# Attention and two gated MLPs on one core: the work list of the first two blocks is written anew

## The chip, the cores and the metric

The kernel runs on one core of a Trainium2 chip. The metric is the time of one execution on the device in microseconds (us). Before the change three runs gave 1640.0, 1640.85 and 1644.39 us, a median of 1640.85 us.

## What is computed

```python
def _attn_ref(q, k, v, g_norm):                    # 8 x 8 heads, 576 positions, 64 wide
    kv = np.einsum('bhsd,bhse->bhde', k, v)        # "k'v": one 64x64 matrix per head
    out = np.einsum('bhsd,bhde->bhse', q, kv)
    rms = np.sqrt(np.mean(out * out, axis=-1, keepdims=True) + 1e-06)
    return out / rms * g_norm
def _moe_ref(x, w_gate, w_val, w_out):             # 4608 tokens, 512 -> 1536 -> 512
    return (1 / (1 + np.exp(-(x @ w_gate))) * (x @ w_val)) @ w_out
def _moe2_ref(x, w_in, w_out):                     # 512 -> 2048 -> 512
    h = x @ w_in
    return np.where(h >= 1, h, np.where(h <= -1, 0, (h + 1) ** 2 / 4)) @ w_out
```

The reference applies the three one after the other. The weights of the two MLPs come as float64.

## The kernel before

The 4608 tokens are worked through in 9 blocks of 512. A block is held with the 512 features on partitions, as four tiles of 128x512, one for each pair of heads. Large products are exact to float32 with a trick: both operands are split into a high and a low half, and three products (high-high, high-low, low-high, `mm3`, lines 92 to 96) are added in PSUM.

For a block the attention goes like this. `kv_heads` multiplies k by v for the pairs (128-position chunks, 64x64 results), the result is copied to SBUF (`kvw`), `attn_two` multiplies it with q to X, two tiles of 128x512 in PSUM. The squares of X are summed over each head, the sums become reciprocal roots (the norm), these are spread again over 64 partitions by a small product (`scale_steps`, result R), and x = X times g_norm times R is split into halves. The first MLP then multiplies x with 12 columns of weights `f`; each column has a gate half and a value half (`gv_chunk`, four chunks of three products each), and the sigmoid of the gate times the value is stored in DRAM.

The first two blocks (0 and 1) are special. Nothing can be hidden behind earlier work there, so the steps of both blocks, the decoding of the first three weight columns from float64 (`dec`, six VectorE steps per tile) and the first products are written out by hand as a list of names, `order` in the text. Each name is a generator, and each time that it stands in the list one step of it is issued. `kv10` is k'v of block 1, pair 0; `X10` is X of block 1, pairs 0 and 1; `sq`, `sum`, `norm`, `turn`, `scale`, `split` are the steps of the norm; `W0110` is weight column 0, block 1, value half (1), chunk 0; `g01` is the sigmoid of column 0, block 1. Every engine runs its own instructions strictly in the order in which they are issued, so the list sets which instruction of an engine stands behind which.

The first block's norm and the second's are made differently before the change. For block 0 the squares are multiplied, as the stationary operand, with a matrix of two columns (`early_sums`, line 285): four products of two columns for each pair, tokens on partitions, so that the six steps of the norm work on 32 columns. `early_turn` (line 308) turns the 8 rows back. For block 1 the squares are split into halves (`half`), multiplied with a 0/1 matrix `gather` (`middle_squares`, line 323, two products of 512 columns per pair), and the norm steps work on 512 columns (`middle_norm`).

The inputs are loaded through one queue, SyncE's (SP), in the order of the text: block 0's k, v, rest, q for each pair, then the weights of column 0, block 1's, then columns 1 and 2. A load waits for the eighth load before it. POOL's queue stores the split weights to DRAM (`store_resident`) for later stages, where they are read back. After the list, a loop over `f` = 1 to 11 runs columns 1 to 11 for block 1 and 2 to 11 for block 0 (`first`), while VectorE decodes column f+2.

Of the kernel before, what the change touches and what calls it, by code (L numbers as in the profile page):

```python
# [15 lines left out]
P = 128  # L16
# [17 lines left out]
def attn_gated_mlp_kernel(ctx: ExitStack, tc: tile.TileContext, a: dict, out: bass.AP):  # L34
# [273 lines left out]
    def early_turn(j):  # L308
        rt = bank("R", 1, "rt", (H, T))
        for c in range(TC):  # L310
            nc.tensor.matmul(rt[:, c * P:(c + 1) * P], state[j][:, c, :], eye, start=True, stop=True)
        yield
        hi, lo = (tp.tile([H, T], F32R, name=f"rt_{n}", tag=n) for n in ("sqh", "sql"))
        yield from split_steps(rt, hi, lo)
        state[j] = hi, lo
# [141 lines left out]
    def store_resident(f):  # L457

        d = w1d[f]
        store_halves(wgv[f, 0], [d[:, 0:2, h] for h in range(2)])  # L460
        store_halves([t[:, 2 * P:] for t in wgv[f, 1]], [d[:, 2, h] for h in range(2)])
# [94 lines left out]
    def store_halves(halves, dst):  # L556
        for t, d in zip(halves, dst):
            t = t.bitcast(F32)
            nc.gpsimd.dma_start(out=d, in_=t if len(d.shape) == 2 else t.rearrange("p (o n) -> p o n", n=2 * P))  # L559
# [495 lines left out]
    with tc.manual_schedule():  # L1055
# [57 lines left out]
        square_tags = (("sq", "sqh", "gf", "sig"), ("gf", "sig", "nm", "nr"))  # L1113
        high_tags, low_tags = ("nt", "woh", "woh", "sq"), ("wol", "wol", "qraw", "qraw")
        two = ("woh", "wol", "qraw")
        gv_banks = {(0, 0): (None, None), (1, 0): (2, 1), (0, 1): (None, None)}

        class Early:

            def kv(b, p):  # L1120
                if p % 2 == 0:
                    kvb[b, p // 2] = at_p.tile([P, 2, D], F32, name="kvps", tag="at")
                kv_heads(kvb[b, p // 2], b, p)
# [10 lines left out]
            def X(b, i):  # L1134
                attn_two(b, i, None if b == i == 1 else [acc_tile(c, "X") for c in ((0, 1) if i else (2, 3))])
# [10 lines left out]
            def half(b, p):  # L1146
                hi, lo = (half_tile(tp, "sqh", t[p], bufs=2 if t[p] in two else 1) for t in (high_tags, low_tags))
                yield from split_steps(state[b, p], hi, lo)
                state[b, p] = hi, lo
# [11 lines left out]
            def scale(b, p):  # L1161
                bank = acc_tile((0, 3)[p] if b else p % 2, "R") if b == 0 or p < 2 else at_tile("R")
                yield from scale_steps(b, p, bank, state["x", b, p])
# [22 lines left out]
            def W(f, b, i, c):  # L1186
                if c == 0:
                    gb[f, b, i] = gv_bank(i, gv_banks[f, b][i])
# [19 lines left out]
        def feed(n):  # L1208
# [6 lines left out]
            kv00 kv01 kvw00 X00 sq00 x00 sq01 x01 kv02 sum00 kv03 kvw01 X01 dec00 cast dec00 dec00 sum01 dec00 sq03 sq02 x02  # L1215
            dec01 dec00 sum02 dec00 dec01 w00 dec01 dec01 sum03 kv10 norm0 norm0 kv11 norm0 dec01 norm0 dec01 norm0 kvw10
            norm0 w01 w00 turn0 x03 w01 X10 turn0 turn0 scale00 sq11 x10 scale01 half11 scale00 kv12 sq10 scale01 scale02
            kv13 split00 half11 kvw11 split00 half10 X11 scale02 split01 dec10 half10 W0010 sq13 split01 sum10 sq12 dec10
            W0000 dec10 half12 sum11 dec10 half13 scale03 half12 split02 half13 dec11 sum12 dec10 sum13 dec11 dec10 W0001
            split02 w10 norm1 W0011 dec11 norm1 w10 W0002 norm1 scale03 W0012 norm1 split03 norm1 W1000 dec11 split03 W1001  # L1220
            norm1 dec11 norm1 dec11 W1002 norm1 W0003 w11 W0013 scale10 w11 W1003 x11 W1010 scale10 scale11 x12 g00 W1011
            scale11 split10 dec20 scale12 split11 W1012 split10 scale12 x13 dec21 scale13 W1013 split12 g00 g10 W0100
            split11 W0110 scale13 W0101 split12 split13 W0111 split13 W0102 g10 W0112 dec20 W0113 dec20 dec21 W0103 dec21
            dec20 g01 dec20 dec20 g01 w20 dec21 dec21 w20 dec21 w21 w21
# [335 lines left out]
```

## Time and profile before

| | |
|---|---|
| median of three runs | 1640.85 us (1640.0 to 1644.39) |
| the profiled execution | 1640.12 us; its span, first to last instruction, 1638.3 us |
| TensorE matmul (PE) busy | 1621.2 us, 99% of the span |
| VectorE (DVE) / ScalarE (ACT) / GpSimd (POOL) busy | 71% / 55% / 11% |
| TensorE clock, mean | 0.996 of full speed |
| last product of weight columns 0 for block 1 ends, and block 2's first k'v starts | 66.93 us from the start |

The span counts from the first instruction to the last one; the execution's own time has 1.8 us more around it. A busy time of PE says only that a product was under way. All of the change lies in the first 70 us.

### The profile page before, as it was taken

Reading aid. Unit: us, or ns where it says so; the run is one execution under the profiler, and the core shown is the slowest. Engines: PE = TensorE matmul, PEld = TensorE weight load, DVE = VectorE, ACT = ScalarE, POOL = GpSimd, SP = SyncE. Lnnn points to the kernel's source line nnn. Section 1 sums busy time; section 2 is a strip of 40 time slices with the busy share of each in tenths; the row PEclk is TensorE's granted clock in tenths of the full one; section 3 lists DMA queues with packets and bytes.
Section 4 is the critical chain, followed back from the end, with each engine's and each line's share of the span. In section 5 each row is a group of like instructions: output and inputs, shape, how many; then the busy total and the mean of one; then the engine's idle time right before and its main releaser. Section 6 shows DMA issues by size and latency. Waiting matters only on the chain.

```text
span 1638.3 us, 22607 instructions
## 1 busy us (share of the span) xinstructions
PE 1621.2 (99%) x8060; PEld 1355.5 (83%) x8060; DVE 1159.8 (71%) x1726; ACT 901.9 (55%) x1384; POOL 186.7 (11%) x292
## 2 busy tenths in 40 slices
PE   8999999999999999999999999999999999999999
PEld 6778878887788777788888788888888888999999
DVE  5987876786786667676666646965795588479476
ACT  3444445765774457744433456646754675575563
POOL 0112042211211111210221100000000000000000
PEclk8999999999999999999999999999999999999999
DMA  9676797678985998859985876558655755777855
GB/s 286 213 262 234 225 317 255 203 270 299 364 320 175 330 330 318 284 195 332 349 307 192 286 272 232 186 190 297 201 199 204 277 186 202 286 274 260 320 179 193
DMA packets 146575, 422.07 MB, mean 258 GB/s; under 512 B 18200, under 2 KB 25496, under 8 KB 132384
## 3 DMA queue, kind: packets, MB, share of 16 engines
q1 hardware_dynamic: 125536, 353.51, 63.9%
q0 software_dynamic: 20928, 67.13, 11.0%
q8 instruction: 64, 1.05, 0.3%
q14 instruction: 47, 0.39, 0.1%
HBM read 337.20 MB, written 83.36 MB: 257 GB/s over the span
## 4 chain that ended last, share of the span: by engine, by line
PE 62%; issue 26%; POOL 6%; DMA 3%; DVE 2%; ACT 1%; SPq 0%; POOLq 0%; DVEq 0%; ACTq 0%
PE bank L836 21%; PE bank L996 21%; PE pA L672 5%; PE acc L96 3%; PE acc L94 3%; PE acc L95 3%; PE pF L672 2%; POOL w1d L559 2%; POOL w2d L559 1%; POOL wo2d L559 1%; PE pD L672 1%; PE h L94 1%; PE h L95 1%; PE h L96 1%; DMA woh<-wo1d 1%
## 5 line engine op out<-in xcount | busy, mean ns | idle before, releaser
L996 PE MATMUL bank<-gh,wo 128*128 128x512 f32 (+1 forms) x1680 | 345.8, 367 | 0.0
L996 PEld LDWEIGHTS bank<-gh,wo 128*128 128x128 f32 x1680 | 305.8, 188 | 39.2
L69 ACT ACTIVATE gh<-g 128x1024 fp32r<-128x1024 f32 (+2 forms) x171 | 155.5, 912 | 135.8 <-PE bank L996 99.2
L672 PE MATMUL pA<-xc,wc 128*128 128x512 f32 x828 | 212.0, 391 | 1.9 <-ACT pD L69 1.3
L836 PE MATMUL bank<-x_t,wst 128*128 128x512 f32 (+1 forms) x960 | 210.0, 367 | 0.0
L836 PEld LDWEIGHTS bank<-x_t,wst 128*128 128x128 f32 x960 | 175.2, 188 | 22.4
L672 PEld LDWEIGHTS pA<-xc,wc 128*128 128x128 f32 x828 | 154.4, 188 | 36.6 <-ACT pD L69 2.6
L771 DVE TENSOR_TENSOR gh<-g,gh 128x1024 fp32r<-128x1024 f32 (+1 forms) x140 | 156.0, 1115 | 29.7 <-ACT gh L69 29.4
L69 ACT ACTIVATE kept<-bank 128x512 f32<-128x512 f32 (+1 forms) x200 | 109.3, 549 | 95.2 <-PE bank L836 82.0
L94 PE MATMUL acc<-gh,woh 128*128 128x512 f32 x404 | 158.2, 392 | 2.9 <-DMA woh<-wo1d 2.3
L836 PE MATMUL bank<-x_b,wst 128*128 128x512 f32 (+1 forms) x720 | 160.8, 367 | 0.0
L771 DVE TENSOR_TENSOR g<-bank,kept 128x512 f32<-128x512 f32 (+1 forms) x160 | 98.1, 634 | 84.4 <-ACT kept L69 45.8
L95 PE MATMUL acc<-gl,woh 128*128 128x512 f32 x404 | 157.5, 390 | 0.1
L836 PEld LDWEIGHTS bank<-x_b,wst 128*128 128x128 f32 x720 | 131.5, 188 | 16.9
L886 DVE SCALAR_TENSOR_TENSOR g<-r,g 128x1024 f32<-128x1024 f32 (+1 forms) x70 | 78.0, 1114 | 73.1 <-ACT r L883 73.1
L96 PE MATMUL acc<-gh,woh 128*128 128x512 f32 x308 | 120.2, 390 | 0.0
L880 ACT ACTIVATE r<-g,half 128x1024 f32<-128x1024 f32 (+1 forms) x70 | 74.4, 1064 | 65.3 <-DVE g L771 65.3
L672 PE MATMUL pF<-xc,wc 128*128 128x512 f32 x432 | 109.7, 389 | 0.0
L672 PEld LDWEIGHTS pF<-xc,wc 128*128 128x128 f32 x432 | 81.0, 188 | 17.2 <-issue 0.4
L94 PEld LDWEIGHTS acc<-gh,woh 128*128 128x128 f32 x404 | 75.8, 188 | 20.7 <-ACT nm L69 1.4
L95 PEld LDWEIGHTS acc<-gl,woh 128*128 128x128 f32 x404 | 75.8, 188 | 16.1 <-DVE gl L77 0.5
L771 DVE TENSOR_TENSOR g<-g 128x1024 f32<-128x1024 f32 (+1 forms) x80 | 88.6, 1113 | 0.5
(221 smaller groups left out, 2559.2 us busy)
## 6 DMA issues: line engine op xcount, KB each, us to landing
wo<-wo2d SPq DMA_DIRECT2D x70, 1024.0 KB, 5.0
wc<-w1d SPq DMA_DIRECT2D x252, 256.0 KB, 5.5
woh<-wo1d SPq DMA_DIRECT2D x162, 256.0 KB, 5.4
wst<-w2d SPq DMA_DIRECT2D x40, 1024.0 KB, 5.5
wst<-w2d SPq DMA_DIRECT2D x40, 768.0 KB, 4.5
raw<-in_w SPq DMA_DIRECT2D x32, 512.0 KB, 6.0
raw<-in_w_gv SPq DMA_DIRECT2D x24, 512.0 KB, 5.4
w1d<-w2half POOLq DMA_DIRECT2D x48, 256.0 KB, 4.4
```

Of the source, the lines that this page charges most:

```text
L69: nc.scalar.activation(out=o, in_=i, func=AF.Copy)
L94: nc.tensor.matmul(ps, w[0][:, wsl], x[0], start=first, stop=False)
L95: nc.tensor.matmul(ps, w[0][:, wsl], x[1], start=False, stop=False)
L96: nc.tensor.matmul(ps, w[1][:, wsl], x[0], start=False, stop=last)
L559: nc.gpsimd.dma_start(out=d, in_=t if len(d.shape) == 2 else t.rearrange("p (o n) -> p o n", n=2 * P))
L672: nc.tensor.matmul(o, w[:, h, sl], x[c][l], start=first and c == n == 0, stop=c == 1 and n == 2, skip_group_check=True)
L771: nc.vector.tensor_tensor(out=o, in0=x, in1=y, op=op)
L836: nc.tensor.matmul(bank, self.ws[w][h][:, sl], self.xo[x][:, l, c], start=first and c == n == 0, stop=c == 1 and n == 2, skip_group_check= ...
L880: nc.scalar.activation(out=r, in_=v, func=AF.Relu, bias=self.half, scale=0.5)
L886: nc.vector.scalar_tensor_tensor(out=v, in0=r, scalar=1.0, in1=v, op0=ALU.min, op1=ALU.max)
L996: nc.tensor.matmul(bank[i][o], self.wo2[2 * i + k // 2][:, k % 2 * 2 + e, h, o * P:(o + 1) * P], ops[m][:, l, e], start=first, stop=k == H ...
```

## The change

Five things change, all at the beginning. (1) The list of names stands in another order. (2) The sums of block 1's squares are made as block 0's are, with `early_sums`, `early_norm` and `early_turn`; `half`, `middle_squares` and `middle_norm` are no longer used for block 1. (3) X is copied out of PSUM, times g_norm, by ScalarE in place of VectorE, for six of the eight pairs. (4) k and v of one pair come in one load into the ring `raw` of six buffers, which the raw weights share. (5) k'v of block 1 is made for two pairs at a time, with the products of the two pairs alternating. Besides, the banks of PSUM are given out differently (column 0 and column 1 of block 0 both use h1 and h0), and the four stores of weight column 0 move from POOL's queue to SP's; there they are issued in the loop after the list, as before in the text.

```diff
     def load_kv_early(b, p):
-        k, v, r = (wp.tile([P, T], F32, name="kv_early", tag="w") for _ in range(3))
-        k, v = (x[0:SC].rearrange("p (c n) -> p c n", c=NSC) for x in (k, v))
-        r = r[0:SR, 0:2 * P].rearrange("p (i n) -> p i n", i=2)
-        nc.sync.dma_start(out=k, in_=a["kv_main"][b, p][:, 0])
-        nc.sync.dma_start(out=v, in_=a["kv_main"][b, p][:, 1])
+        t = tp.tile([SC, 2, NSC, P], F32, name="kvraw", tag="raw", bufs=6)
+        nc.sync.dma_start(out=t, in_=a["kv_main"][b, p])
+        r = wp.tile([P, T], F32, name="kv_early", tag="w")[0:SR, 0:2 * P].rearrange("p (i n) -> p i n", i=2)
         nc.sync.dma_start(out=r, in_=a["kv_rest"][b, p])
-        kvraw[b, p] = k, v, r
+        kvraw[b, p] = t[:, 0], t[:, 1], r
...
-        nc.vector.tensor_scalar(out=x, in0=X, scalar1=gn, scalar2=None, op0=ALU.mult)
+        if j == 0 and p < 2:
+            nc.vector.tensor_scalar(out=x, in0=X, scalar1=gn, scalar2=None, op0=ALU.mult)
+        else:
+            nc.scalar.activation(out=x, in_=X, func=AF.Copy, scale=gn)
...
-            state[j] = bank("R", 0, "SSt", (P, TC, H))
+            state[j] = bank("R", 2 * j, "SSt", (P, TC, H))
...
-        rt = bank("R", 1, "rt", (H, T))
+        rt = bank("R", 1 + j, "rt", (H, T))
...
     def store_resident(f):
         d = w1d[f]
+        queue = nc.gpsimd if f else nc.sync
...
-        gv_banks = {(0, 0): (None, None), (1, 0): (2, 1), (0, 1): (None, None)}
+        scale_banks = (("h0", "at", "at", "h0"), ("at", "at", 0, 1))
+        gv_banks = {(0, 0): ("h1", "h0"), (0, 1): (0, 1), (1, 0): ("h1", "h0")}
...
-                kv_heads(kvb[b, p // 2], b, p)
+                kv_heads(kvb[b, p // 2], b, *((p, p + 1) if b else (p,)))
...
-                (middle_squares if b else early_sums)(b, p)
+                early_sums(b, p)
...
-                yield from (middle_norm if b else early_norm)(b)
+                yield from early_norm(b)
...
-            kv00 kv01 kvw00 X00 sq00 x00 sq01 x01 kv02 sum00 kv03 kvw01 X01 dec00 cast dec00 dec00 sum01 dec00 sq03 sq02 x02
+            kv00 kv01 kvw00 X00 kv02 x01 sq00 sq01 x00 kv03 sum00 kvw01 dec00 X01 dec00 dec00 sum01 sq02 dec00 sq03 sum02
...
```

Three places of the new order matter for what follows. The first is TensorE's queue around the first block's norm: `SSt` are the two-column sums of squares, `rt` is the turn, `R` the spread, `kvps` is k'v, `X` the attention product. Before:

```order
L290 MATMUL SSt<-ones_169,sq 128x2 x12
L159 MATMUL kvps<-kv_early 64x64 x20
L311 MATMUL rt<-eye,early_r 8x128 x4
L186 MATMUL X<-q_early,kvw_174 64x64 x4
L186 MATMUL X<-q_early,kvw_175 64x448 x4
L319 MATMUL R<-rt_sqh,spread 128x512
L319 MATMUL R<-rt_sql,spread 128x512
```

And now:

```order
L291 MATMUL SSt<-ones_169,sq 128x2 x12
L312 MATMUL rt<-eye,early_r 8x128 x4
L157 MATMUL kvps<-kvraw 64x64 x8
L157 MATMUL kvps<-kv_early 64x64 x2
L157 MATMUL kvps<-kvraw 64x64 x8
L157 MATMUL kvps<-kv_early 64x64 x2
L320 MATMUL R<-rt,spread 128x512 x8
L184 MATMUL X<-q_early,kvw_174 64x64 x4
L184 MATMUL X<-q_early,kvw_175 64x448 x4
L94 MATMUL h<-xh_455,w 128x512
```

The turn now stands ahead of block 1's first k'v, all four spreads follow at once, and X of block 1 comes after them; the first weight product is the next thing.

The second place is TensorE's queue where the weight products (`h`) begin. Before, block 1's squares are summed there with `SSh`, of 512 columns:

```order
L94 MATMUL h_538<-xh_511,w 128x512
L95 MATMUL h_538<-xl_512,w 128x512
L96 MATMUL h_538<-xh_511,w 128x512
L328 MATMUL SSh<-sqh,gather 128x512 x2
L94 MATMUL h_551<-xh_511,w 128x512
L95 MATMUL h_551<-xl_512,w 128x512
L96 MATMUL h_551<-xh_511,w 128x512
L328 MATMUL SSh<-sqh,gather 128x512 x2
L319 MATMUL R<-rt_sqh,spread 128x512
L319 MATMUL R<-rt_sql,spread 128x512
L328 MATMUL SSh<-sqh,gather 128x512 x4
```

Now the sums are `SSt`, and the second X of block 1 stands among them:

```order
L291 MATMUL SSt<-ones_169,sq 128x2 x4
L184 MATMUL X<-q_early,kvw_174 64x64 x4
L184 MATMUL X<-q_early,kvw_175 64x448 x4
L291 MATMUL SSt<-ones_169,sq 128x2 x4
L94 MATMUL h<-xh_473,w 128x512
L95 MATMUL h<-xl_474,w 128x512
L96 MATMUL h<-xh_473,w 128x512
L291 MATMUL SSt<-ones_169,sq 128x2 x8
```

The work of block 1 up to its sums has moved behind the first weight products.

The third place is TensorE's queue at the first product of weight column 1 (the rows show the numbers of the tiles and what an instruction waits for). Before, it writes `h0_613`, a bank of its own, while columns 0 are in `h0_551` and `h1_538`:

```order
L94 MATMUL h1_538<-xh2_569,w_445 128x512
L95 MATMUL h1_538<-xl2_570,w_445 128x512
L96 MATMUL h1_538<-xh2_569,w_446 128x512
L94 MATMUL h0_613<-xh0_511,w_587 128x512 [waits Activation_49]
L95 MATMUL h0_613<-xl0_512,w_587 128x512
L96 MATMUL h0_613<-xh0_511,w_588 128x512 [waits DVE_49]
```

And now (`h_625` is the gate of column 1; it takes the bank of `h_480`, the gate of column 0):

```order
L312 MATMUL rt_597<-eye_172,early_r_576 8x128 [waits DVE_49,PE_49]
L312 MATMUL rt_597<-eye_172,early_r_576 8x128 x3
L94 MATMUL h_480<-xh3_541,w_391 128x512
L95 MATMUL h_480<-xl3_542,w_391 128x512
L96 MATMUL h_480<-xh3_541,w_392 128x512
L94 MATMUL h_515<-xh3_541,w_448 128x512
L95 MATMUL h_515<-xl3_542,w_448 128x512
L96 MATMUL h_515<-xh3_541,w_449 128x512
L94 MATMUL h_625<-xh0_455,w_565 128x512 [waits Activation_49]
```

The first product of column 1 now stands two chunks behind the second turn and waits for ScalarE. On ScalarE the copy of the turn, a table load and the sigmoid that reads `h_480` follow each other:

```order
L284 ACTIVATE xb<-X,gn 128x512
L69 ACTIVATE rt<-rt 8x512
L1194 ACT_TABLE_LOAD
L1194 ACTIVATE sig<-h 128x512
L69 ACTIVATE w<-dt 128x512
```

The sigmoid that frees the bank stands right behind the copy and the table load.

## Rows read from the trace of the kernel before

**Rows 1.** Windows: length, busy PE, PEld, DVE, ACT, POOL, then PEclk, DMA, GB/s.

```profile
20.00:30.00 10.00, 8.16 (x59) 7.09 (x59) 6.77 (x14) 2.23 (x7) 2.03 (x3) 0.52 1.06 279
...
40.00:50.00 10.00, 9.12 (x36) 6.17 (x36) 9.86 (x18) 5.99 (x10) 1.76 (x3) 1.00 0.56 162
...
70.00:80.00 10.00, 10.00 (x64) 8.13 (x64) 8.31 (x14) 3.85 (x7) 2.81 (x4) 1.00 1.03 336
```

**Rows 2.** Waits of PE, first 67 us: waiting line, releaser, us, times, longest.

```profile
PE kvps L159 <- DMA kv_early<-in_kv_main: 3.3, 3, 1.5
```

**Rows 3.** Waits of PE from 67 us to the end, the longest.

```profile
PE acc L94 <- DMA woh<-wo1d: 2.3, 3, 1.0
```

**Rows 4.** Timeline of PE, 15 to 30 us: start, duration, instructions.

```profile
15.21 1.35 PE L159 MATMUL kvps<-kv_early 112*64 112x64 f32 x20
...
16.92 1.09 PE L186 MATMUL X<-q_early,kvw 64*64 64x512 f32 x8 [0.37 <-ACT kvw L69]
17.94 1.05 PE L290 MATMUL SSt<-ones,sq 128*128 128x2 f32 x8
19.27 2.57 PE L290 MATMUL SSt<-ones,sq 128*128 128x2 f32 x16 [0.27 <-ACT sq L278]
22.59 2.36 PE L159 MATMUL kvps<-kv_early 112*64 112x64 f32 x20 [0.74 <-DMA kv_early<-in_kv_main]
26.04 2.37 PE L159 MATMUL kvps<-kv_early 112*64 112x64 f32 x20 [1.09 <-DMA kv_early<-in_kv_main]
28.34 1.88 PE L311 MATMUL rt<-eye,early_r 128*8 128x128 f32 x8
```

**Rows 5.** Timeline of DVE: first and last step of block 0's norm.

```profile
23.28 0.18 DVE L295 TENSOR_SCALAR early_m<-SSt 128x32 f32<-128x32 f32 x1
...
24.74 0.18 DVE L305 TENSOR_TENSOR early_r<-early_r,early_t 128x32 f32<-128x32 f32 x1
```

**Rows 6.** Timeline of PE, 35 to 69 us.

```profile
35.78 1.53 PE L186 MATMUL X<-q_early,kvw 64*64 64x64 f32 x16
37.24 0.50 PE L94 MATMUL h<-xh,w 128*128 128x512 f32 x1
...
54.48 0.73 PE L319 MATMUL R<-rt,spread 8*128 8x512 f32 x2
55.14 0.50 PE L94 MATMUL h<-xh,w 128*128 128x512 f32 x1
...
55.94 0.39 PE L94 MATMUL h<-xbh,w 128*128 128x512 f32 x1
...
66.93 0.69 PE L159 MATMUL kvps<-kvraw 112*64 112x64 f32 x16
...
68.24 0.50 PE L94 MATMUL h<-xh,w 128*128 128x512 f32 x1
```

**Rows 7.** Windows of 2 us between 20 and 42 us, columns as in Rows 1.

```profile
20.00:22.00 2.00, 1.84 (x11) 1.75 (x11) 1.97 (x4) 0.24 (x2) 0.00 (x0) 0.60 1.04 258
...
30.00:32.00 2.00, 2.00 (x21) 1.05 (x20) 1.13 (x2) 1.03 (x2) 0.67 (x2) 0.84 1.06 387
...
34.00:36.00 2.00, 2.00 (x24) 1.53 (x23) 1.27 (x3) 0.12 (x1) 0.00 (x0) 1.00 1.01 410
...
40.00:42.00 2.00, 2.00 (x9) 1.39 (x9) 2.00 (x5) 1.00 (x2) 0.00 (x0) 1.00 0.98 212
```

**Rows 8.** Timeline of POOL: first store of weight column 0.

```profile
22.82 0.83 POOL L559 DMA_DIRECT2D w1d<-w  x1 [20.44 <-ACT w L69]
```

**Rows 9.** Timeline of ACT: table load and first sigmoid.

```profile
49.41 1.28 ACT L1194 ACT_TABLE_LOAD   x1
50.70 0.60 ACT L1194 ACTIVATE sig<-h 128x512 f32<-128x512 f32 x1
```

**Rows 10.** Timeline of DVE: halves of weight column 4.

```profile
87.10 1.28 DVE L77 TENSOR_TENSOR w<-dt,w 128x512 fp32r<-128x512 f32 x2
```

**Rows 11.** Timeline of PE: products of block 0, column 4, begin.

```profile
92.79 0.50 PE L94 MATMUL h<-xh,w 128*128 128x512 f32 x1
```

More of the change, by code (lines that the diff above doesn't have):

```diff
@@ L312, in early_turn @@
         yield
-        hi, lo = (tp.tile([H, T], F32R, name=f"rt_{n}", tag=n) for n in ("sqh", "sql"))
+        hi, lo = (tp.tile([H, T], F32R, name="rt", tag=n, bufs=2 if n == "qraw" else 1) for n in (("sqh", "sql"), ("sq", "qraw"))[j])
         yield from split_steps(rt, hi, lo)
@@ L459, in store_resident @@
         d = w1d[f]
-        store_halves(wgv[f, 0], [d[:, 0:2, h] for h in range(2)])
-        store_halves([t[:, 2 * P:] for t in wgv[f, 1]], [d[:, 2, h] for h in range(2)])
+        queue = nc.gpsimd if f else nc.sync
+        store_halves(wgv[f, 0], [d[:, 0:2, h] for h in range(2)], queue)
+        store_halves([t[:, 2 * P:] for t in wgv[f, 1]], [d[:, 2, h] for h in range(2)], queue)
     def w1_steps(f):
@@ L554, in w2_steps, with store_halves @@
         yield from halves_out(u1, lambda h: d[:, 5:7, h])
-    def store_halves(halves, dst):
+    def store_halves(halves, dst, queue=nc.gpsimd):
         for t, d in zip(halves, dst):
             t = t.bitcast(F32)
-            nc.gpsimd.dma_start(out=d, in_=t if len(d.shape) == 2 else t.rearrange("p (o n) -> p o n", n=2 * P))
+            queue.dma_start(out=d, in_=t if len(d.shape) == 2 else t.rearrange("p (o n) -> p o n", n=2 * P))
     def stream_wo(f, tiles=None):
@@ L1112, in attn_gated_mlp_kernel, with early_bank @@
         xa, gb, kvb, norm = {}, {}, {}, {}
-        square_tags = (("sq", "sqh", "gf", "sig"), ("gf", "sig", "nm", "nr"))
-        high_tags, low_tags = ("nt", "woh", "woh", "sq"), ("wol", "wol", "qraw", "qraw")
-        two = ("woh", "wol", "qraw")
-        gv_banks = {(0, 0): (None, None), (1, 0): (2, 1), (0, 1): (None, None)}
+        square_tags = (("sq", "sqh", "gf", "sig"), ("gf", "nm", "nr", "nt"))
+        scale_banks = (("h0", "at", "at", "h0"), ("at", "at", 0, 1))
+        gv_banks = {(0, 0): ("h1", "h0"), (0, 1): (0, 1), (1, 0): ("h1", "h0")}
+        def early_bank(n, name):
+            if n == "at":
+                return at_tile(name)
+            return bank("R", int(n[1]), name) if isinstance(n, str) else acc_tile(n, name)
         class Early:
@@ L1134, in X @@
             def X(b, i):
-                attn_two(b, i, None if b == i == 1 else [acc_tile(c, "X") for c in ((0, 1) if i else (2, 3))])
+                attn_two(b, i, [acc_tile(c, "X") for c in ((0, 1) if i else (2, 3))])
                 yield
@@ L1144, in x @@
                 yield
[L1146 to L1149, printed above, removed]
             def sum(b, p):
-                (middle_squares if b else early_sums)(b, p)
+                early_sums(b, p)
                 yield
             def norm(b):
-                yield from (middle_norm if b else early_norm)(b)
+                yield from early_norm(b)
             def turn(b):
@@ L1161, in scale @@
             def scale(b, p):
-                bank = acc_tile((0, 3)[p] if b else p % 2, "R") if b == 0 or p < 2 else at_tile("R")
-                yield from scale_steps(b, p, bank, state["x", b, p])
+                yield from scale_steps(b, p, early_bank(scale_banks[b][p], "R"), state["x", b, p])
             def split(b, p):
@@ L1187, in W @@
                 if c == 0:
-                    gb[f, b, i] = gv_bank(i, gv_banks[f, b][i])
+                    gb[f, b, i] = early_bank(gv_banks[f, b][i], "h")
                 gv_chunk(gb[f, b, i], f, i, xs if b else xa, c)
@@ L1214, in attn_gated_mlp_kernel @@
         order = """
-            kv00 kv01 kvw00 X00 sq00 x00 sq01 x01 kv02 sum00 kv03 kvw01 X01 dec00 cast dec00 dec00 sum01 dec00 sq03 sq02 x02
[L1216 to L1224, printed above, removed]
+            kv00 kv01 kvw00 X00 kv02 x01 sq00 sq01 x00 kv03 sum00 kvw01 dec00 X01 dec00 dec00 sum01 sq02 dec00 sq03 sum02
+            dec00 dec01 dec00 x02 sum03 norm0 dec01 norm0 norm0 norm0 dec01 norm0 w00 norm0 dec01 turn0 x03 w00 cast dec01
+            kv10 turn0 turn0 dec01 kvw10 scale00 scale02 scale00 w01 scale01 scale02 split00 scale03 X10 scale01 split00
+            split01 w01 split02 W0000 sq10 scale03 kv12 sq11 split02 dec10 split01 W0010 kvw11 dec10 sum10 dec10 dec11 X11
+            dec10 split03 dec11 dec10 sum11 sq12 W0001 sq13 dec11 dec10 x10 sum12 dec11 w10 sum13 W0011 norm1 w10 norm1
+            norm1 W0002 norm1 split03 norm1 W0012 dec21 norm1 dec11 turn1 x12 dec21 W0003 dec11 turn1 W0013 dec21 g00 turn1
+            w11 W1000 g00 x13 scale10 w11 x11 W1001 scale10 dec20 W1010 dec21 split10 W1002 dec20 W1011 dec21 W1003 dec20
+            scale12 dec21 W1012 dec20 w21 scale11 scale12 g10 W1013 split10 scale13 scale11 W0100 scale13 split11 dec20
+            split11 W0110 dec20 W0101 w21 w20 split12 w20 split13 W0111 split12 W0102 split13 g10 W0103 W0112 g01 W0113 g01
         """
```

## The prediction

> **What bounds the kernel now.** I read the windows first. Late in the start PE is busy in every microsecond of a window while DVE, the next busiest, keeps some time free (8.31 of 10 at 70 us); before 50 us PE loses time, and between 20 and 30 us its clock is 0.52 of full speed [rows 1]. The waits say the same: in the first 67 us PE lost 3.3 us to loads of k and v [rows 2], and in the 1570 us after that its longest wait in total is 2.3 us [rows 3]. So from some 50 us on the kernel is one queue of products. Whatever the change does, it is worth what it moves the point at which PE enters that queue: I take the start of block 2's first k'v, 66.93 us [rows 6], behind which the order is as it was. If it starts 1 us earlier, the kernel ends 1 us earlier, unless a load or a weight is late further on.
>
> The front in detail. Pair 3 of block 0 is multiplied at 15.21, when its v has landed. The sums of squares end at 19.27 + 2.57 = 21.84. The norm begins only at 23.28, since DVE was decoding weights, and ends at 24.92 [rows 5]. The turn would then be ready, but it stands behind two k'v products that wait for loads, so it runs at 28.34 [rows 4]. After that come spread, X of block 1 and, at 37.24, the first weight product [rows 6].
>
> **The change part by part: the start of the weight products.** I follow the new order with the old durations. The loads: k and v of a pair in one, same bytes. At 20 to 22 us the separate loads of k, v, the rest and q are under way, at 258 GB/s. The trace has a row for the joint form too: at 40 to 42 us the loads under way are block 2's k, v and rest, which already come that way, and they move 212 GB/s; weights at 34 us move 410 [rows 7]. The bounds are 212 and 410; I take the old rate, since the joint form itself has the row nearest to it. By the Trainium skill (DMA: Bandwidth & Descriptors, Rules for kernel authors) many small transfers should be coalesced into a large one. By that rule the pairs would come faster; by the row nothing is gained, and the rule's case is the second rival.
>
> So pair 3 still starts at 15.1 and ends at 16.5. The sum of pair 0 now stands behind it and covers the copy of k'v: 17.6. X 1.1: 18.7; the sum of pair 1, 1.05: 19.7; the last two sums 2.57: 22.3. The six steps of the norm now meet a DVE that waits for them: 24.92 - 23.28 = 1.64 us: 23.9, one microsecond earlier. The turn stands ahead of k'v: 25.8 instead of 30.2. Pairs 0 and 1 of block 1 landed by 26.04, and without the 256 KB stored at 22.82 [rows 8] perhaps 0.9 us sooner: no wait is left. Two pairs alternating took 68.24 - 66.93 = 1.3 us for block 2, as much as one alone; at the low clock one took 2.37, so I take 2.4: 28.3. Eight spreads: 0.23 each at full clock (a pair of products and the gap 55.14 - 54.48 = 0.66): 1.9 to 2.6, so 30.4. X of block 1, 37.24 - 35.78 = 1.46: 31.8. The x halves (multiplication, ScalarE's copy, subtraction, 0.6 to 0.7 each, with two other multiplications between) are ready at about 31.5. **The first weight product moves from 37.24 to about 31.7, a gain of 5.5 us.** Bounds: 27.5, if pairs land at 410 GB/s (448 KB are 458,752 bytes: 1.8 us at 258, 1.1 at 410, so each of the four pairs comes 0.7 us sooner, 2.8 together) and the clock is full again earlier, 1.4 us less for k'v and the spreads; 32.7, if the clock stays at half until X is done.
>
> **What stands behind it.** Before, 66.93 - 37.24 = 29.7 us follow. Now more follows, because k'v, X and the sums of block 1 stand there:
> - weight products: 24 chunks of the list and 8 of the loop. 16 chunks take 66.93 - 55.94 = 10.99, 0.69 each: 21.9
> - k'v of pairs 2 and 3 of block 1: 1.4. X of those: 1.5
> - two-column sums: four times 1.05 [rows 4] and 0.1 for each change of operand: 4.6
> - the second turn: 1.88 at half clock [rows 4], so about 1.0 at full
> - four spreads, 0.66 and two gaps of 0.09: 0.84 each: 3.4
> - a new wait. The gate of column 1 takes the bank of the gate of column 0. It cannot start before the sigmoid, which stands behind the turn's copy and a table load: 0.6 (as the sigmoid) + 1.28 + 0.60 = 2.5 us after the turn [rows 9]; PE has two chunks to do in that time, 1.4. So 1.1 us of waiting; behind the waiting product all of PE's queue stands
>
> The sum is 34.9 us, 5.2 more than before. 31.7 + 34.9 = 66.6: **0.3 us earlier than 66.93.** The front's gain is spent behind it.
>
> **What is hidden.** DVE loses six X copies, four splittings of squares and four wide operations of the norm: 14 operations of 0.64 us (two take 1.28 [rows 10]), 9 us. They were on DVE while it was 9.86 of 10 us busy at 40 to 50 us [rows 1]. PE's waits there were under 2 us, so their removal is not 9 us but those waits, and I have replaced them by the table's wait. The rest of DVE's list, some 17 us after the last sum (27 operations of 0.64 us), ends a little before PE wants its last halves; it is nearly as long as PE's own 20 us. On ScalarE the six copies (about 0.6 each, as the sigmoid) go into idle time (ACT 5.99 of 10). The four stores of column 0 (768 KB) move from 22 to 31 us to some 70, where DMA is full (1.03) [rows 1]. At the 336 GB/s of that row they cost 2.3 us of DMA time, and SP's later weight loads stand behind them. The nearest consumer is column 4: its halves end at 88.4 [rows 10], PE asks for them at 92.79 [rows 11], so 4.4 us cover the 2.3. If the cover is gone, it costs what is over.
>
> The sum in the profiled execution is 1640.12 - 0.3; the median is 0.7 above that execution. From the median: 1640.5.
>
> **The rivals.**
> - *The clock falls in block 1's sums; slower.* Between 18 and 21.8 us PE was on the two-column sums, and the clock fell to 1.2 GHz in the window at 20 (mean 0.60), and was full again only after 30 [rows 7], when PE had been on k'v, turn and X without a pause since 26. The new list puts two such sums next to each other with only one or two weight chunks on either side. If the clock falls there for 4 us, the products take 2 us more; if for the 10 us seen in the front, 5 us more: 1642 to 1645.5, most likely 1643. It decides from about 1 us, that is a fall of 2 us. Against it: between these sums PE has full weight products, which the front hadn't. By the Trainium skill (TensorE: Matmul & The Clock Gate, What's actually happening) activity releases the throttle, so a PE that is always busy, as here, would not fall; in the trace it fell while the sums were shown as busy.
> - *The joint loads are faster; clearly faster.* 410 GB/s instead of 258 gives a start at 27.5: 62.4, so 4.5 us gained, 1636.4. For it: the weights' row at 410 with rows of the same 4 KB. Against it: the row at 212 of the very same load.
> - *The stores at 70 us make column 4 late; slower.* PE waits at 92.79 if the weights come over 4.4 us later. Two delays would have to add up: 1642.
> - *It doesn't do what it says.* The norm still waits for pair 3 of block 0, whose landing the list doesn't move; if spread or X of block 1 find another wait, the products start at 34 and the end is 2 us later: 1642.5.
>
> **How the numbers follow.** The forecast, both sides repaid: 0.53, 1640.5, with 1638.5 to 1642.5 as its own range. Clock falls: 0.19. Faster loads: 0.17. Late weights: 0.05. Another wait: 0.06. A measurement of this kernel can tell 0.3% from no change, 4.9 us: faster means below 1635.9, slower above 1645.8. Faster: half of the second rival, whose centre lies at 4.5 us, and some of the forecast's tail, since the bounds of the loads are far apart: 0.14. Slower: a quarter of the first and a little of the last two, 0.07. The rest, 0.79, is within 0.3%. The range goes from 1634.5, a little past the second rival, to 1645.5, the end of the first.
>
> **What would show it.** In the changed kernel's trace: the turn at about 24 us, ahead of k'v; the first weight product near 31.7 (27.5 would be the second rival, 34 the last); a PE wait of about 1 us for the sigmoid behind the second turn; a granted clock of 1.00 from 31 to 50 us (a window at 0.5 would be the first rival); block 2's k'v at 66 to 67 us. I am wrong if that k'v starts before 62 or after 71, or if PE then shows a wait for weights that it did not have.

## The result, and the profile after

The changed kernel takes 1648.9 us (median of 5 runs, 1647.87 to 1651.65). The kernel before took 1640.85 beside it, so the ratio is 1.0056 [1.004, 1.0072]: slower by about 8 us. The forecast was 1640.5, the range 1634.5 to 1645.5. The prediction is wrong.

The profiled execution took 1647.87 us, its span 1646.1, which is 7.8 more than before. Block 2's first k'v, which stood at 66.93 [rows 6], now starts at 73.91. So 7.0 of the 7.8 us are lost in the first 74 us. The timeline of TensorE (PE) in the changed kernel, first part, answers to [rows 4] (start, duration, instructions, idle before and releaser):

```profile
16.02 0.68 PE L157 MATMUL kvps<-kvraw 112*64 112x64 f32 x8 [1.46 <-DMA kvraw<-in_kv_main]
...
19.34 4.00 PE L291 MATMUL SSt<-ones,sq 128*128 128x2 f32 x24
24.91 1.86 PE L312 MATMUL rt<-eye,early_r 128*8 128x128 f32 x8 [1.56 <-issue]
26.70 1.59 PE L157 MATMUL kvps<-kvraw 112*64 112x64 f32 x15
...
28.30 1.05 PE L157 MATMUL kvps<-kvraw 112*64 112x64 f32 x14
...
29.61 3.78 PE L320 MATMUL R<-rt,spread 8*128 8x512 f32 x8
33.31 1.99 PE L184 MATMUL X<-q_early,kvw 64*64 64x64 f32 x16
35.23 0.79 PE L94 MATMUL h<-xh,w 128*128 128x512 f32 x1
```

The order is the predicted one: turn ahead of k'v, one block of spreads, X, then the first weight product. But the product starts at 35.23, not at 31.7, and the rows before it are as long as at half clock: eight spreads 3.78, X 1.99 (at full clock, in e1, 2.23 and 1.10). The second part, which answers to [rows 6]:

```profile
42.98 1.86 PE L291 MATMUL SSt<-ones,sq 128*128 128x2 f32 x16
...
48.51 1.04 PE L312 MATMUL rt<-eye,early_r 128*8 128x128 f32 x8
...
52.13 0.50 PE L94 MATMUL h<-xh,w 128*128 128x512 f32 x1 [0.99 <-ACT sig L1194]
...
73.91 0.69 PE L157 MATMUL kvps<-kvraw 112*64 112x64 f32 x16
```

The wait for the sigmoid is there with 0.99 us (1.1 had been expected). The waits of PE in the first 75 us, as in [rows 2]:

```profile
PE kvps L157 <- DMA kvraw<-in_kv_main: 3.1, 2, 1.6
PE rt L312 <- issue: 1.6, 1, 1.6
...
PE h L94 <- ACT sig L1194: 1.0, 1, 1.0
...
PE h L94 <- ACT xbh L69: 0.4, 1, 0.4
```

With those left out they are 8.1 us, 1.6 more than before. What differs most is the clock. Windows of 10 us of the changed kernel (length, busy PE, PEld, DVE, ACT, POOL, then PEclk, DMA share, GB/s; as in [rows 1]):

```profile
20.00:30.00 10.00, 8.33 (x69) 7.06 (x69) 6.68 (x14) 4.40 (x12) 0.00 (x0) 0.54 1.07 247
30.00:40.00 10.00, 10.00 (x77) 6.40 (x76) 7.07 (x13) 5.23 (x10) 0.00 (x0) 0.61 0.85 279
40.00:50.00 10.00, 10.00 (x65) 7.73 (x66) 5.64 (x13) 4.47 (x11) 1.56 (x2) 0.83 0.75 236
```

Before, the window at 40 had 1.00 [rows 1] and the clock was full by 32 [rows 7]. Now it stays at 1.2 GHz until 37.8 and falls once more, from 44.7 to 48.1. Added up over windows of 0.5 us, PE spent 23.9 us of the first 75 at half clock, before 13.7.

### The profile page after: what moved, and what is told of

It reads as the page before. It is cut to its first block, busy times and chain, and to the rows that moved or that the text cites. A ratio compares the mean times of both kernels' runs of the same rounds, so it can differ in the third digit from the quotient of the medians.

```text
span 1646.1 us, 22650 instructions
## 1 busy us (share of the span) xinstructions
PE 1627.4 (99%) x8092; PEld 1358.0 (83%) x8092; DVE 1151.8 (70%) x1716; ACT 900.8 (55%) x1386; POOL 183.4 (11%) x288
## 4 chain that ended last, share of the span: by engine, by line
PE 61%; issue 27%; POOL 6%; DMA 3%; DVE 1%; ACT 1%; SPq 0%; POOLq 0%; DVEq 0%; ACTq 0%
PE bank L838 21%; PE bank L998 21%; PE pA L674 4%; PE acc L96 2%; PE acc L94 2%; PE acc L95 2%; POOL w1d L561 2%; PE pF L674 2%; POOL w2d L561 1%; POOL wo2d L561 1%; PE h L94 1%; DMA kvraw<-in_kv_main 1%; PE h L95 1%; PE h L96 1%; PE pD L674 1%
```

## Experiments

In the changed kernel single parts were undone (e2, e6, e9, e11, e16) or helped (e1, e3, e4, e5), or several at once (e7, e8, e13); in the kernel before one part was done alone (e14), waits were filled (e10, e12) or lateness was made (e15). Two parts were never undone: the alternating k'v of two pairs and the banks of PSUM. c1 and c2 are the two kernels themselves, profiled once more. In the table, "half, all" is the time at half clock averaged over all executions of that kernel, 2 x (1 - mean granted clock) x span (for the kernel before, the 74 executions run beside the experiments). It also counts later falls: the profiles of e12, e2, e3 and e4 hold one of 3.4 us at 244, 594, 600 and 935 us. "half, profile" is that of the profiled one before 75 us; "k'v" the start of block 2's first k'v; "rest" the span behind it.

| run | median us | half, all | half, profile | k'v | rest |
|---|---|---|---|---|---|
| before | 1640.85 | 14.6 | 13.7 | 66.93 | 1571.4 |
| c1 before again | 1640.92 | 15.1 | 13.7 | 67.21 | 1571.9 |
| changed | 1648.9 | 26.4 | 23.9 | 73.91 | 1572.2 |
| c2 changed again | 1649.67 | 23.9 | 30.7 | 75.32 | 1574.5 |
| e1 norm's wait filled | 1648.7 | 19.8 | 13.7 | 71.00 | 1575.1 |
| e2 loads apart | 1649.71 | 19.8 | 17.1 | 70.17 | 1578.0 |
| e3 sums apart | 1650.61 | 27.2 | 30.7 | 75.39 | 1577.6 |
| e4 table early, new tile | 1654.35 | 24.0 | 17.1 | 71.53 | 1583.1 |
| e5 table early, in place | 1648.2 | 23.9 | 20.5 | 71.76 | 1573.7 |
| e6 stores on POOL | 1650.21 | 23.8 | 20.5 | 70.34 | 1575.4 |
| e7 = e1 + e2 + e5 | 1645.91 | 18.4 | 17.1 | 68.33 | 1573.8 |
| e8 = e7 + e6 | 1646.68 | 22.2 | 23.9 | 70.72 | 1575.5 |
| e9 old second norm | 1649.46 | 26.4 | 23.9 | 75.37 | 1572.5 |
| e10 before, two waits filled | 1641.3 | 11.5 | 10.2 | 66.04 | 1573.1 |
| e11 k'v in norm's wait | 1650.48 | 22.3 | 17.1 | 72.96 | 1572.8 |
| e12 before, front filled | 1640.2 | 9.6 | 6.8 | 66.03 | 1572.0 |
| e13 changed, front filled | 1645.26 | 12.1 | 6.8 | 66.03 | 1574.6 |
| e14 before, joint loads | 1642.82 | 18.6 | 17.1 | 67.81 | 1570.8 |
| e15 before, made late | 1650.47 | 14.8 | 10.2 | 72.80 | 1574.3 |
| e16 X by VectorE | 1648.37 | 23.1 | 20.5 | 70.74 | 1573.0 |

**e1.** Four unused wide products in the wait for the first norm.

```
+            def busy(n):
+                ps = h_p.tile([P, T], F32, name="unused", tag="h1")
+                for _ in range(n):
+                    nc.tensor.matmul(ps, ones, gather.rearrange("p n q -> p (n q)"), start=True, stop=True)
+                yield
-            x02 sum03 norm0 dec01
+            x02 sum03 busy4 norm0 dec01
```

> The changed kernel with four products of 512 columns (constant operands, result unused) put on TensorE between the sums of squares of block 0 and the turn, where TensorE waited 1.56 us for the norm. Clock theory (the clock stays at 1.2 GHz from 20.7 to 37.7 us because TensorE does little in the sums and then waits, and this costs most of what was lost): the clock is full again before 31 us, k'v, spread and X of block 1 take 5 to 7 us instead of 8.6, the first weight product starts at 31.5 to 33 instead of 35.23, block 2's first k'v at 70 to 71.5 instead of 73.91, time 1645 to 1647. Load theory (k and v come late in one load): nothing moves, the added 1.7 us at half clock fill the wait, first weight product 35.2 to 35.5, time 1649. List theory (waits of the new order): as the load theory.

The k'v that the clock theory expected came (71.00, 2.9 us sooner than in the changed kernel), its time did not: 1648.7, ratio 1.0057 [1.0042, 1.0072] to before. The rest is longer by as much.

**e2.** k and v of a pair in two loads again.

```
-        t = tp.tile([SC, 2, NSC, P], F32, name="kvraw", tag="raw", bufs=6)
-        nc.sync.dma_start(out=t, in_=a["kv_main"][b, p])
+        nc.sync.dma_start(out=k, in_=a["kv_main"][b, p][:, 0])
+        nc.sync.dma_start(out=v, in_=a["kv_main"][b, p][:, 1])
```

> The changed kernel with k and v of the first two blocks loaded apart again, into buffers of their own, as before the change; all else as changed. Load theory: pair 3 of block 0 starts at 15.2 instead of 16.02, the norm ends 0.8 us sooner, and since a step of the clock may be met, all behind it by 0.8 to 4 us: block 2's first k'v at 70 to 73, time 1645 to 1648. Clock theory: pair 3 0.8 us sooner, the clock still at half until 34 or later, block 2's k'v at 72.5 to 73.5, time 1648. List theory: the same as the clock theory.

Pair 3 started at 15.61, half of the way back, and the first k'v came at 70.17; the time stayed: 1.0059 [1.0044, 1.0074]. The rest, 1578.0, holds the fall of the clock at 594 us.

**e3.** Two of block 1's two-column sums moved apart.

```
-            w10 sum13 W0011 norm1
+            w10 W0011 sum13 norm1
```

> The changed kernel with the last two-column sum of block 1 put behind the next weight chunk, so that no two sums follow each other. Clock theory: the clock, which fell from 44.7 to 48.0, stays full there; 1.5 us are won, less the norm's being 0.7 us later: block 2's first k'v at 72 to 73, time 1647 to 1648. If the sums have nothing to do with that fall: it falls at the same place and the k'v comes at 74 to 74.7, time 1649 to 1650.

The second fall, at 44 us, is gone in its profile, but the first one lasted from 9 to 40 us; 1.0062 [1.0045, 1.0079]. The profile cannot price the sums: the front alone varied more, and its rest holds a fall at 600 us.

**e4 and e5.** A tiny sigmoid ahead of the second turn loads its table early. e4 writes it to a new one-column tile, e5 over an old one.

```
+            def table():
+                nc.scalar.activation(out=half, in_=half, func=AF.Sigmoid)
+                yield
-            dec21 norm1 dec11 turn1
+            dec21 norm1 table dec11 turn1
```

> The changed kernel with a sigmoid of one column issued on ScalarE ahead of the copy of the second turn, so that the table load of 1.28 us falls into ScalarE's wait for the turn. List theory: the wait of 0.99 us for the sigmoid ahead of column 1 goes, VectorE's work behind it comes 1.2 us sooner, and the two later waits (0.4 and 0.3) shrink: block 2's first k'v at 72.3 to 73, time 1647.5. Clock theory: the same by itself, since it owns only the other 5 us; if the k'v comes later than 73.5, the waits behind fill up what is won.

> The sigmoid's table is loaded by a tiny sigmoid ahead of the turn, as in e4, but the sigmoid now writes over an old one-column tile, so no tile moves in SBUF. Address theory (a moved tile slowed the products in e4): 512-column products at 389 ns again instead of 395. Front theory (what is lost by 70 us is lost for good, what is won there is won): block 2's first k'v at about 71.5 us as in e4, the end 2.4 us earlier than in the changed kernel, 1646.5 us. Absorbing theory (waits between 186 and 920 us take a front gain back): first k'v at 71.5, but 1648 to 1650 us.

In both the wait for the sigmoid is gone, and in neither the time: e5 1.0054 [1.0038, 1.007], e4 1.0087 [1.0066, 1.0108]. The two differ by 4 bytes of SBUF in each partition, allotted ahead of all later tiles. Groups of weight products of e4 between 100 and 185 us (instructions, busy us, mean ns of one, idle before):

```profile
L96 PE MATMUL h<-xl,w 128*128 128x512 f32 x58 | 22.9, 395 | 0.0
L97 PE MATMUL h<-xh,w 128*128 128x512 f32 x58 | 22.9, 395 | 0.0
```

The same groups of e5:

```profile
L95 PE MATMUL h<-xl,w 128*128 128x512 f32 x61 | 23.8, 390 | 0.0
L96 PE MATMUL h<-xh,w 128*128 128x512 f32 x61 | 23.8, 389 | 0.0
```

The same products at the same clock and without a wait take 5 to 6 ns more each in e4. Its median is 6.2 us longer. Its rest is 9.4 us longer (1583.1 against 1573.7), but 3.4 us of that rest, at 935 us, were at half clock.

**e6.** Column 0's halves stored from POOL again.

```
-        queue = nc.gpsimd if f else nc.sync
+        queue = nc.gpsimd
```

> Column 0's weight halves are stored from POOL's queue again, all else as changed. Stores theory (the stores moved to SP's queue are what makes the waits of 186 to 262 us longer, 1.3 us in the changed kernel, and the ones up to 600 us): waits of that stretch back to 1.2 us in all, 1646 to 1647.5 us. Front theory: no change at 74 us, none behind it, 1648.5 to 1649.5 us.

No gain: 1.0071 [1.0049, 1.0093]. Undoing the moved stores gives nothing back.

**e7 and e8.** The mends of e1, e2 and e5 together; e8 has that of e6 too.

> Three mends together: four unused products in the wait for the norm, k and v loaded apart, sigmoid's table loaded early and in place. Front theory: block 2's first k'v at 66 to 68 us, 1641 to 1643 us. Absorbing theory (later waits grow by what the front gives): first k'v at 66 to 68, but 1645 to 1649 us, with the growth visible between 186 and 800 us.

> e7 with column 0's weight halves stored from POOL's queue again. Stores theory: 2 to 5 us under e7, near the kernel before (1640 to 1642 us). Front theory: as e7 within 1 us. If neither mend of the front nor the stores brings the time under 1645 us, the loss behind 186 us belongs to the new order of the list itself.

e7 is the first that gives something back: 1645.91, 1.0043 [1.0028, 1.0059], about 3 us. e8 is the same within the spread, 1.0046 [1.0029, 1.0062]. Neither came under 1645 us, which had been set down beforehand as the sign that the new order itself loses time behind the front.

**c1 and c2.** Both kernels once more, unchanged.

> The kernel before, unchanged, profiled a second time. Order theory (the changed list makes the waits of 186 to 262 us 1.3 to 2.9 us longer, as in every variant so far): block 2's first k'v at 66.5 to 67.5 us, waits of 1.0 to 1.4 us on TensorE between 185 and 265 us, 1571 to 1572 us from that k'v to the end. Chance theory (the first profile of before was a lucky one behind 186 us): 2 to 4 us of waits there and 1573 to 1577 us behind the first k'v.

> The changed kernel, unchanged, profiled a second time. If the half-clock stretch belongs to the changed order alone: again about 24 us at half clock before 75 us and block 2's first k'v at 73.5 to 74.5 us. If it falls differently in each execution: half clock anywhere from 14 to 31 us in all, first k'v from 70 to 76 us.

The front of before repeats: half clock again in two stretches at 10 and 20 us, 13.7 us in all, k'v at 67.21, rest 1571.9. That of the changed kernel does not. Its second profile, same windows as above:

```profile
20.00:30.00 10.00, 8.44 (x40) 6.36 (x40) 4.68 (x12) 3.99 (x9) 0.00 (x0) 0.50 1.06 235
30.00:40.00 10.00, 10.00 (x111) 6.96 (x110) 8.34 (x16) 4.70 (x9) 0.00 (x0) 0.67 0.91 293
40.00:50.00 10.00, 10.00 (x67) 7.71 (x66) 6.36 (x15) 5.38 (x12) 1.57 (x2) 0.84 0.74 224
```

Here the clock was at half from 9 to 33, and again at 36 and 46. So one profile of this front is a sample, and differences of 2 us in k'v or in the rest (1572.2 and 1574.5) between the runs above say little by themselves; the averages over all executions say more.

**e9.** The second norm as before (halves of the squares, eight wide products, no turn).

```
-                early_sums(b, p)
+                (middle_squares if b else early_sums)(b, p)
-                yield from early_norm(b)
+                yield from (middle_norm if b else early_norm)(b)
```

> The changed kernel with the second norm as before (squares split in halves, eight wide products for the sums, no turn). Clock theory (two-column sums bring the clock down a second time): no fall between 40 and 48 us, first k'v 1.5 to 3 us earlier than in the changed kernel (71 to 72.5 us), 1646 to 1647.5 us. Rival (the two-column norm is no part of the loss): 1648 to 1651 us, the halves' copies on ScalarE and VectorE making up for the shorter sums.

The rival holds: 1649.46, 1.0047 [1.0032, 1.0062]. The clock fell at 48 us all the same, and the sigmoid was waited for 2.5 us. Undoing the two-column norm gives nothing back, and that its sums make the clock fall is not shown.

**e10.** Unused products in two waits of the kernel before.

```
-            sum03 kv10 norm0 norm0 kv11
+            sum03 busy2 kv10 norm0 norm0 busy3 kv11
```

> The kernel before with two and three unused 512-column products in TensorE's two waits for k and v of block 1 (at 22 and 25 us). Clock theory (a wait with wide products in it ends the half-clock stretch sooner, as in e1): half clock up to 27 us instead of 30.6, first k'v 1 to 2 us earlier (65 to 66 us), 1638.5 to 1640 us beside 1640.5. Rival (the loads of block 1 set the time there, and unused products only push them back): first k'v at 67 to 68 us and 1640.5 to 1642 us.

The front came as the clock theory expected (half clock to 27.3, k'v 0.9 us sooner), its time did not: 1.0004 [0.9991, 1.0017].

**e11.** Block 1's first k'v ahead of the norm, as before.

```
-            x02 sum03 norm0 dec01
+            x02 sum03 kv10 norm0 dec01
...
-            kv10 turn0 turn0 dec01 kvw10
+            turn0 turn0 dec01 kvw10
```

> The changed kernel with block 1's first k'v (two pairs) ahead of the norm again, as in the kernel before, in place of behind the turn. Theory of the wait (the empty wait for the norm, with narrow work on both sides, draws the half-clock stretch out): half clock about 14 us in all before 75 us, as in the kernel before, block 2's first k'v at 68 to 70 us, 1643 to 1645 us. Rival (the moved place is no part of it, and the product now waits for its loads until 26 us and holds the turn back): half clock 20 us or more, first k'v at 73 to 76, 1648 to 1651 us.

The rival holds in wait and time: 1650.48, 1.0058 [1.004, 1.0076]; the time at half clock, 17.1, lies between the two. The product now waits for its loads, and the turn behind it. PE in e11:

```profile
23.26 0.48 PE L157 MATMUL kvps<-kvraw 112*64 112x64 f32 x2
27.07 1.01 PE L157 MATMUL kvps<-kvraw 112*64 112x64 f32 x13 [3.33 <-DMA kvraw<-in_kv_main]
```

**e12 and e13.** Unused products all over the front: 16 in the kernel before (the expectation miscounts them as 15 in seven places), 17 in the changed one, which also has the mends of e2 and e5. Two places of the kernel before:

```
-            kv00 kv01 kvw00 X00
+            kv00 busy4 kv01 kvw00 busy1 X00
...
-            dec00 dec00 sum01 dec00
+            dec00 dec00 sum01 busy1 dec00
```

> The kernel before with 15 unused 512-column products in seven places of its front up to 26 us. Clock theory (wide products in the waits keep the clock up): half clock 0 to 7 us instead of 14, block 2's first k'v at 63.5 to 65.5 us, 1636 to 1639 us. Rival (the loads of block 1 end at 25 us whatever the clock does, and behind them the clock rises anyway): first k'v at 66 to 68, 1640 to 1642 us.

> The changed kernel with k and v loaded apart, the sigmoid's table loaded early, and 17 unused 512-column products in seven places of its front. Clock theory: half clock 0 to 10 us, first k'v at 63 to 66 us, 1638 to 1642 us, so most of the loss is back. Rival (what the clock gives is lost again in the later waits): first k'v at 63 to 66 but 1644 to 1646 us. Second rival (narrow work behind the turn brings the clock down whatever stood before it): half clock 10 us or more, all of it behind 27 us, first k'v at 67 to 69.

PE in e13:

```profile
21.17 1.84 PE L1141 MATMUL unused<-gather,ones 128*128 128x512 f32 x4
23.07 1.88 PE L314 MATMUL rt<-eye,early_r 128*8 128x128 f32 x8
24.88 1.39 PE L159 MATMUL kvps<-kv_early 112*64 112x64 f32 x40
26.19 2.27 PE L322 MATMUL R<-rt,spread 8*128 8x512 f32 x8
28.39 1.99 PE L186 MATMUL X<-q_early,kvw 64*64 64x64 f32 x16
30.31 0.79 PE L94 MATMUL h<-xh,w 128*128 128x512 f32 x1
...
66.03 0.69 PE L159 MATMUL kvps<-kvraw 112*64 112x64 f32 x16
```

With less time at half clock, and with the mends, the front comes out near what the prediction had worked out: k'v of two pairs 1.4, spreads 2.3, the first weight product at 30.31, k'v at 66.03. The time is 1645.26, 1.0037 [1.0021, 1.0053], as the first rival had it. That is 3.6 us better than the changed kernel, and still 5 us worse than e12 (1640.2, 1.0005 [0.9992, 1.0018]), whose profile has the same k'v. The clock does not explain these 5 us: the executions with a mean granted clock of 0.997 or more, eight of each, have the same mean clock (0.998) and take 1644.4 us in e13 and 1639.8 in e12. Nor did e12 gain: on average it spends 5.0 us less at half clock than the kernel before, worth about 2 (0.35 to 0.46 us each, worked out below), and its unused products take at least 16 x 0.2275 = 3.6 us of PE, partly out of waits. No version beat the kernel before.

**e14.** Joint loads alone, in the kernel before.

```
-        nc.sync.dma_start(out=k, in_=a["kv_main"][b, p][:, 0])
-        nc.sync.dma_start(out=v, in_=a["kv_main"][b, p][:, 1])
+        t = tp.tile([SC, 2, NSC, P], F32, name="kvraw", tag="raw", bufs=6)
+        nc.sync.dma_start(out=t, in_=a["kv_main"][b, p])
```

> The kernel before with one load for k and v of a pair, nothing else changed. Theory of the joint load (its data land together, so k'v of a pair starts 0.8 us later, as in the changed kernel): first k'v of block 2 0.5 to 1.5 us later (67.5 to 68.5), 1641 to 1642.5 us. Rival (a load of twice the size uses the queues better): 0.5 to 1.5 us earlier, 1639 to 1640 us. If half clock grows to 20 us here too, the joint load is what moves the clock.

k'v 0.9 us later, as expected, but with 3.4 us more at half clock ahead of it, so this is not the load's own price. Pair 3 of block 0 started at 16.28 in place of 15.21. The ratio is 1.001 [0.9998, 1.0021], -0.3 to 3.4 us, with 4.0 us more at half clock on average.

**e15.** The kernel before with 31 unused products ahead of the first weight product.

```
-            dec10 half10 W0010 sq13
+            dec10 half10 busy9 busy9 busy9 busy4 W0010 sq13
```

> The kernel before with 31 unused 512-column products in a row ahead of the first weight product, 31 x 0.2275 = 7.05 us, so that its front is as late as the changed one's, at full clock and in the old order. Lateness theory (TensorE 7 us later against the loads and stores is what lengthens the later waits): first k'v at 73 to 74 us, 1574 to 1577 us from there to the end, 1648 to 1651 us. Order theory (the changed list itself does it): first k'v at 73 to 74, 1571 to 1573 us behind it, 1646 to 1648 us.

In the profile k'v is 5.9 us late and the end 8.8, so 2.9 us come behind k'v, in the old order and at full clock; the rest of 1574.3 is 1.2 to 3.5 us above those of the five profiles of this order that are not late (1570.8 to 1573.1). On average the end is 9.8 late (1650.47, 1.0062 [1.0048, 1.0076]). The products took more than the 7.05 us expected, 8.5 with the gaps between them (35.78 to 44.26), so by that only 1.3 us come on top. This speaks for the lateness theory, and its size is not settled. One place can be seen between 185 and 275 us, where ScalarE and VectorE split the output weights and wait until the halves in their buffers are stored. These waits in the kernel before (line, releaser, us, times, longest):

```profile
ACT woh L69 <- DMA wo1d<-woh: 2.9, 4, 1.1
DVE wol L77 <- DMA wo1d<-wol: 0.7, 2, 0.4
```

The same in the changed kernel:

```profile
ACT woh L69 <- DMA wo1d<-woh: 4.7, 6, 1.5
DVE wol L77 <- DMA wo1d<-wol: 4.1, 5, 1.7
```

The same in e15:

```profile
ACT woh L69 <- DMA wo1d<-woh: 6.1, 7, 1.9
DVE wol L77 <- DMA wo1d<-wol: 2.6, 3, 1.3
```

Their sum is 3.6 to 5.4 us in the five profiles of the kernel before and its variants that are not late, 8.7 in e15, and 6.0 to 9.0 in all of the changed list but e13, the one with an early k'v, which has 5.3. Little of it reaches PE: in this stretch PE is idle for 1.3 to 2.3 us in those five profiles, 2.7 in e15 and 2.1 in both of the changed kernel.

**e16.** All X of the first two blocks copied by VectorE.

```
-        if j == 0 and p < 2:
+        if True:
```

> The changed kernel with every X of the first two blocks copied by VectorE again. Theory so far (the copies are no part of the loss): 1647.5 to 1650 us, first k'v within the changed kernel's own 70 to 75 us. Rival (ScalarE, with the copies on it, is what makes the second turn's halves and the sigmoid late): the sigmoid's wait of 1.0 us at 52 us gone, first k'v 1 to 2.5 us earlier, 1645.5 to 1647.5 us.

1648.37, 1.0045 [1.0031, 1.006]; the wait for the sigmoid is still 1.0 us. Undoing the copies gives nothing back that is clear of the noise.

## Why the prediction was wrong

*Two steps failed.* The first is "I follow the new order with the old durations", in the prediction's start of the weight products: it took over, with the durations, the places at which the clock fell and rose. The order came out as worked out. But the same work takes 1.3 us at full and 2.9 at half clock (k'v of two pairs: e13, changed kernel), 2.2 and 3.8 (8 spreads), 1.10 and 1.99 (X), and the new order got more of the half clock than was put in:

- k'v of two pairs 2.4, measured 2.9 (26.70 to 29.61); spreads 1.9 to 2.6, measured 3.7; X 1.46, measured 1.9. Together 2.6 of the 3.5 us by which the first weight product missed 31.7. Even the bound of 32.7, the clock at half until X is done, was too low, since it kept 2.6 as the most that spreads can cost.
- Pair 3 "still starts at 15.1": it started at 16.02. That is the other 0.9. k and v land together; with joint loads in the old order it started at 16.28 (e14), with two loads in the new order at 15.61 (e2), but with joint loads in e6 at 15.42, so the size varies from execution to execution. The Trainium skill (DMA: Bandwidth & Descriptors, Rules for kernel authors) advises to coalesce many small transfers; loads of 224 KB gained nothing by it here (e14).
- Behind the first product, 34.9 expected and 38.7 measured (73.91 - 35.23). The clock was still at half to 37.8, which costs 1.2 us, and for 3.4 us at 44.7, 1.6 us; two waits for block 1's last halves (0.4 and 0.3) were not in the list; the sigmoid was there (0.99 for 1.1).

The second is "If it starts 1 us earlier, the kernel ends 1 us earlier". In e13 block 2's first k'v starts 0.9 us earlier than in the kernel before, and the profiled execution ends 2.2 us later (1642.33 against 1640.12), the median 4.6 later (1645.26 against 1640.67 beside it). In e15 5.9 us became 8.8.

*How much of the loss is which.* Over 84 executions of the kernel before (c1 among them) and 9 of the changed one, the means are 1640.5 and 1649.5, the mean granted clocks 0.9955 and 0.9923. That is 14.6 and 25.3 us at half clock. By the spreads, X and the 24 sums of block 0 (2.84 us at full clock in e6, 5.28 at half in c2) a microsecond at half costs 0.41 to 0.46; among the 84 executions themselves one more at half goes with 0.35 us more of time. So the 10.7 more are an estimated 3.7 to 4.9 of the 9.0 us, and 4.1 to 5.3 are not the clock; that fits the 4.6 by which e13 and e12 differ at the same clock. Where these lie is shown in part only. Ahead of that k'v TensorE is idle for 8.1 and 7.5 us in the two profiles of the changed kernel, 6.7 and 6.4 before. Behind it, the rest is 1573.9 us on average in the 11 profiles of the changed list without a later fall of the clock or a moved tile (all but e2, e3 and e4), 1571.8 in the four of the old list that are not late and have no later fall; idle time of TensorE is 1.0 of these 2.1 us (12.0 against 11.0). Being late may lengthen it (e15), but e13 was not late. What in the new order does it is open.

*The rivals.* The first, at 0.19, named the clock, which is about half of the loss. It placed the fall in block 1's sums and priced it at 2 to 5 us; a fall there did come in this profile, for 3.4 us, and its counter-argument, that wide products stand between the sums, did not hold here. The larger part is the first fall, which had been taken for given as in before, and which ended 7 us later. Joint loads at 410 GB/s (0.17) did not come: 247 GB/s between 20 and 30 us. The late stores (0.05) were undone in e6 without effect. The last (0.06) had looked at pair 3 of block 0, which came 0.9 late, but spreads and X found no wait of their own. The prediction's own sign of being wrong, that k'v after 71, was met at 73.91.

*What stays open* is also why the clock comes back so late. Wide products in the norm's wait (e1) and separate loads (e2) each brought the average at half clock from 25.3 to 19.8 us, over four executions each, without a gain in time; a part of the time came back only where both stood together and the table was mended too (e7, e13). The prediction weighed a rule of the Trainium skill (TensorE: Matmul & The Clock Gate, What's actually happening), that activity releases the throttle, and doubted it for the sums. The trace goes further. PE in the changed kernel, windows of 2 us:

```profile
28.00:30.00 2.00, 2.00 (x31) 1.88 (x29) 0.70 (x2) 0.29 (x2) 0.00 (x0) 0.50 1.08 269
30.00:32.00 2.00, 2.00 (x6) 1.50 (x6) 0.97 (x2) 0.93 (x2) 0.00 (x0) 0.50 1.03 220
32.00:34.00 2.00, 2.00 (x16) 1.08 (x18) 1.83 (x4) 0.92 (x3) 0.00 (x0) 0.50 1.05 368
34.00:36.00 2.00, 2.00 (x10) 0.68 (x3) 2.00 (x4) 1.09 (x3) 0.00 (x0) 0.50 1.02 408
```

For 8 us PE is shown as busy without a gap, at 1.2 GHz, with k'v of 64 columns, spreads of 8 rows and X of 64 rows. A full busy column does not tell that the clock is about to rise. The same section of the Trainium skill says that the count of slow products differs between runs of one kernel; the time at half clock does so here in the changed kernel (23.9 and 30.7 us in its two profiles), and not in the two profiles of the one before (13.7 twice).

## What to carry to other kernels

When a list is reordered in a stretch where the clock changes, price it twice, with the rows at half and at full clock, and take the span between the two as the range; the old places of rise and fall do not move along with the instructions. A common queue reached earlier is not yet an earlier end: compare the span behind that point too (e13). Before a loss is put down to the clock, compare executions with the same granted clock; what is left between them is not the clock. And before a difference of 2 us between two profiles is explained, profile the same kernel twice.

## Not expected of the hardware

- A tile of 4 bytes per partition, allotted ahead of the others, made the 512-column products of the weight stage 395 ns in place of 389 or 390 (e4 against e5, 6.2 us in the medians). Why is not shown.
- At the end of eight spreads (8 rows) at full clock, the clock fell while PE was shown as busy without a gap: e13, turn from 23.07, k'v from 24.88, spreads from 26.19 to 28.39. Four wide products had stood ahead of the turn, from 21.17. Windows of 2 us:

```profile
26.00:28.00 2.00, 2.00 (x17) 1.48 (x14) 1.93 (x4) 1.23 (x3) 0.00 (x0) 1.00 1.08 255
28.00:30.00 2.00, 2.00 (x18) 0.52 (x16) 2.00 (x5) 1.44 (x3) 0.00 (x0) 0.56 1.08 302
```
